# Loading the first weights at the fourth unit of attention, and handing out decode and split piece by piece

## The chip, the cores and the metric

The kernel runs on one core of one Trainium2 chip. The metric is the device time of one execution in microseconds (us). Three runs of the kernel before took 1102.81, 1103.84 and 1104.21 us; the median is 1103.84 us.

## The reference

Attention with a cumulative decay bias, causal, over 4 batches, 8 heads, 576 positions and head size 64; its output, as 2304 tokens of 512 values, goes through a gated feed-forward layer (512 to 1536 and back) and then a second one with one input matrix (512 to 2048 and back):

```
cum    = cumsum(max(s, 0))
bias   = -(cum[:, None] - cum[None, :])
scores = q @ k.T / 8 + min(bias, 0), causal mask
attn   = softmax(scores) @ v                      # (4, 8, 576, 64)
x      = attn as (2304, 512)
x      = (silu(x @ w_gate) * (x @ w_val)) @ w_out     # d_ff 1536
out    = silu(x @ w_in) @ w_out2                      # d_ff 2048
```

All is float32. The kernel keeps float32 accuracy on TensorE by splitting each matrix in a high and a low part and running three matmuls for each product (`mm3`: high times high, high times low, low times high).

## The kernel before, in words

**Attention.** A unit is one half ("A": query tiles 0 to 2, "B": tiles 3 and 4) of one head; 64 units in all. `slot_pieces(u)` lists the pieces of work of unit u: the scores and softmax of its tiles, the split of the next head, the load of the head after that, the product with v of unit u-2 and the transposes of unit u-1. The first 18 units (batch 0 and the first head of batch 1) run alone; the rest are mixed into the feed-forward layer, two units to a chunk.

**Feed-forward layers.** The weights come in chunks of 128 x 2048 values. `stream` is the list of chunks: nine for each batch in the first layer (`L1`: six of the gate and value matrices, "gv"; three of the output matrix, "o1"), then eight for the second layer. Each first-layer chunk is 96 matmuls of 288 columns, in 4 steps (gv) or 8 steps (o1). The accumulators of a gate step, the tiles `pgv`, take two of the four PSUM banks of the pool `ps_m`.

**First weights.** The weights arrive in HBM as pairs of 32-bit words, viewed from 64-bit numbers. So a chunk that is met for the first time is loaded as four tiles `r64` of 512 KB each (`w_load`), decoded to float32 (`w_decode`: per tile two ScalarE instructions, lines 413 and 414, and two VectorE instructions, lines 415 and 418), written back to HBM as float32 (`w32`, two stores of 512 KB, line 423), and split in two halves (`w_split`: per half a ScalarE copy to `wh`, line 433 through 113, and a GpSimd subtract to `wl`, line 434). In batches 1 to 3 the chunk is read back from `w32` and only split. The intermediate `dk` of the decode lies in `ps_m` too for the first nine chunks. The tiles `r64` and `wraw` share one pool of five buffers; `wh` and `wl` have four buffers each, two chunks' worth.

**When this is written.** The load, decode and split of chunk 0 and the load of chunk 1 are all written after unit 8 (`PRE = 8`, lines 585 to 589); the load stands behind the loads of the head that was asked for last. In the chunk loop `w_ahead(c)` (lines 568 to 573) writes the whole decode and split of chunk c+1 and the load of chunk c+2 ahead of the first step of chunk c.

**The order on the engines.** The program is written in this order, but a scheduler of the framework places every instruction: it lets instructions that it believes ready go ahead of ones that are written earlier and wait. The result is one fixed order for each engine, which the chip then runs in order: an instruction that waits holds all that stand behind it on its engine. All DMAs are issued from the queue of SyncE (SP).

Of the kernel before, what the change touches and what calls it, by code (L numbers as in the profile page):

```python
# [8 lines left out]
F32 = mybir.dt.float32  # L9
# [8 lines left out]
P = 128  # L18
HB = S // 2
NP = H // 2  # L20
KD = DM // P
# [37 lines left out]
PRE = 8  # L59
# [8 lines left out]
def kernel(  # L68
# [285 lines left out]
    wst = {}  # L354
# [42 lines left out]
    def w_decode(c):  # L397

        raws = []
        for e, t in enumerate(wst[c]):
            lo, hi = t[:, :, 0], t[:, :, 1]
            if e % (CW // 2 // DW) == 0:
                z = raw_p.tile([P, CW // 2], F32, tag="wraw", name="wraw")
                raws.append(z)
            o = e % (CW // 2 // DW) * DW
            zz = z[:, o : o + DW]
            if c < len(L1):
                k = ps_m.tile([P, DW], F32, tag="m", name="dk").bitcast(U32)  # L410
            else:
                k = dec_p.tile([P, DW], U32, tag="dk", name="dk")
            nc.scalar.activation(out=zz, in_=hi.bitcast(F32), func=AF.Copy, scale=2.0**-112)
            nc.scalar.activation(out=k, in_=lo, func=AF.Copy, scale=0.937 * 2.0**-29)  # L414
            nc.vector.scalar_tensor_tensor(  # L415
                out=k, in0=zz.bitcast(U32), scalar=3, in1=k, op0=ALU.logical_shift_left, op1=ALU.bitwise_or
            )
            nc.vector.scalar_tensor_tensor(  # L418
                out=zz.bitcast(U32), in0=hi, scalar=0x80000000, in1=k, op0=ALU.bitwise_and, op1=ALU.bitwise_or
            )  # L420
        for e, z in enumerate(raws if stream[c] in place else []):
            g = place[stream[c]]
            nc.sync.dma_start(out=w32[g, :, e * (CW // 2) : (e + 1) * (CW // 2)], in_=z)
        wst[c] = raws

    def w_split(c):
        if first[c]:
            w_decode(c)
        halves = []
        for t, eng, eng_h in zip(wst[c], WL[phase[c]], WH[phase[c]]):  # L430
            wh = wt_p.tile([P, CW // 2], F32R, tag="wh", name="wh")
            wl = wt_p.tile([P, CW // 2], F32R, tag="wl", name="wl")
            copy(eng_h, wh, t)
            engines[eng].tensor_tensor(out=wl, in0=t, in1=wh.bitcast(F32), op=ALU.subtract)  # L434
            halves.append((wh, wl))
        wst[c] = halves
# [242 lines left out]
```

## Time and profile before

| | |
|---|---|
| median of three runs | 1103.84 us |
| profiled execution: time | 1104.17 us |
| profiled execution: span of the trace | 1102.4 us |
| PE busy | 1073.2 us, 97% of the span |
| DVE, ACT, POOL busy | 705.1 us (64%), 587.2 us (53%), 532.7 us (48%) |
| loads of first weights `r`, 512 KB each | 52 |
| stores `w<-wraw`, 512 KB each | 18 |

The profiled execution lasted 1.8 us longer than its span; what lies outside the span isn't in the trace. A busy PE is one whose matmuls, with modelled ends, cover the time: matmuls overlap, so the row can read full while fewer of them run. The granted clock of TensorE (PEclk) is given as a share of full speed; its two levels are 2.4 GHz and 1.2 GHz. Waits are put down to the instruction whose semaphore came last.

### The profile page before, as it was taken

The numbers are of one execution on the slowest core, as the hardware profiler recorded it, in microseconds if no ns is written. First come the engines' busy times: TensorE is split into PE (matmuls) and PEld (weight loads), VectorE is DVE, ScalarE is ACT, GpSimd is POOL, SyncE is SP. The second block draws the span as 40 slices with busy tenths as digits, with TensorE's granted clock in tenths as the row PEclk, the third lists the DMA queues.
The fourth block names the chain that finished last, engine by engine and source line by source line (L and its number), as shares of the span: only waits on it lengthen the run. The fifth ranks groups of instructions, "written<-read, shape, count | busy, mean of one in ns | idle before, by whom it ended". The sixth has DMA issues, their size and how long they took to land. (4 is left out here: it accounts for less than half of the span.)

```text
span 1102.4 us, 19356 instructions
## 1 busy us (share of the span) xinstructions
PE 1073.2 (97%) x6760; PEld 994.2 (90%) x6760; DVE 705.1 (64%) x1625; ACT 587.2 (53%) x1294; POOL 532.7 (48%) x611
## 2 busy tenths in 40 slices
PE   7979899999999999999999999999999999999998
PEld 4647899999999999999999999888989898888887
DVE  6877788897778886868765346715364645644333
ACT  4887788875766564666645434655243433422221
POOL 7666677675666664757434453232323222332221
PEclk9988999999999999999999999999999999999999
DMA  5587487785353534533144223711010101000012
GB/s 135 137 242 239 157 216 239 210 250 174 86 143 90 140 95 140 149 83 101 39 154 147 77 86 123 226 41 59 20 58 20 58 20 58 20 1 1 1 61 111
DMA packets 53728, 121.39 MB, mean 110 GB/s; under 512 B 8256, under 2 KB 21568, under 8 KB 53632
## 3 DMA queue, kind: packets, MB, share of 16 engines
q1 hardware_dynamic: 53632, 120.17, 36.8%
q8 instruction: 53, 0.87, 0.3%
q14 instruction: 43, 0.35, 0.1%
HBM read 101.20 MB, written 18.95 MB: 109 GB/s over the span
## 5 line engine op out<-in xcount | busy, mean ns | idle before, releaser
L460 POOL TENSOR_TENSOR h<-u,h 128x288 fp32r<-128x288 f32 (+2 forms) x176 | 193.2, 1099 | 349.5 <-ACT h L113 344.7
L445 PE MATMUL po<-h,wh 128*128 128x288 f32 (+2 forms) x704 | 232.8, 332 | 2.1 <-ACT h L113 1.2
L446 PE MATMUL po<-h,wh 128*128 128x288 f32 (+2 forms) x704 | 232.9, 331 | 0.1
L445 PE MATMUL pgv<-xt,wh 128*128 128x288 f32 x768 | 230.9, 301 | 1.4 <-DVE u L458 0.8
L447 PE MATMUL po<-h,wl 128*128 128x288 f32 (+2 forms) x704 | 232.0, 330 | 0.0
L446 PE MATMUL pgv<-xt,wh 128*128 128x288 f32 x768 | 228.8, 298 | 1.5 <-DVE xt L349 1.5
L447 PE MATMUL pgv<-xt,wl 128*128 128x288 f32 x768 | 228.6, 298 | 0.0
L434 POOL TENSOR_TENSOR wl<-wraw,wh 128x1024 fp32r<-128x1024 f32 x53 | 129.2, 2437 | 113.8 <-ACT wh L113 101.5
L113 ACT ACTIVATE h<-u 128x288 fp32r<-128x288 f32 (+2 forms) x176 | 89.4, 508 | 118.0 <-DVE u L458 66.4
L445 PEld LDWEIGHTS pgv<-xt,wh 128*128 128x128 f32 x768 | 144.9, 189 | 3.0 <-DVE u L458 1.1
L446 PEld LDWEIGHTS pgv<-xt,wh 128*128 128x128 f32 x768 | 145.2, 189 | 2.0 <-DVE xt L349 1.8
L447 PEld LDWEIGHTS pgv<-xt,wl 128*128 128x128 f32 x768 | 145.1, 189 | 0.3
L445 PEld LDWEIGHTS po<-h,wh 128*128 128x128 f32 x704 | 132.0, 188 | 10.2 <-ACT h L113 1.8
L456 DVE SCALAR_TENSOR_TENSOR u<-th,pu 128x464 f32<-128x464 f32 (+1 forms) x80 | 50.7, 633 | 137.9 <-ACT th L454 137.9
L447 PEld LDWEIGHTS po<-h,wl 128*128 128x128 f32 x704 | 132.2, 188 | 7.0
L446 PEld LDWEIGHTS po<-h,wh 128*128 128x128 f32 x704 | 132.2, 188 | 6.9 <-POOL h L460 0.5
L540 DVE SCALAR_TENSOR_TENSOR acc<-po,acc 128x464 f32<-128x464 f32 (+1 forms) x140 | 88.5, 636 | 62.6 <-PE po L447 61.9
L454 ACT ACTIVATE th<-pu 128x464 f32<-128x464 f32 (+1 forms) x80 | 44.1, 552 | 152.2 <-PE pu L447 152.2
L113 ACT ACTIVATE wh<-wraw 128x1024 fp32r<-128x1024 f32 x88 | 92.2, 1056 | 52.0 <-PE po L446 27.1
L446 PE MATMUL pu<-x,wh 128*128 128x464 f32 (+1 forms) x320 | 118.9, 371 | 0.0
L445 PE MATMUL pu<-x,wh 128*128 128x464 f32 (+1 forms) x320 | 118.6, 371 | 0.0
L447 PE MATMUL pu<-x,wl 128*128 128x464 f32 (+1 forms) x320 | 118.5, 370 | 0.0
(87 smaller groups left out, 2012.9 us busy)
## 6 DMA issues: line engine op xcount, KB each, us to landing
wraw<-w SPq DMA_DIRECT2D x54, 512.0 KB, 4.8
r<-in_w_dram SPq DMA_DIRECT2D x52, 512.0 KB, 5.0
qkr<-in_qk_dram SPq DMA_DIRECT2D x64, 288.0 KB, 5.1
w<-wraw SPq DMA_DIRECT2D x18, 512.0 KB, 4.4
cumb<-cum_d SPq DMA_DIRECT2D x30, 288.0 KB, 4.1
r<-in_w_dram SPq DMA_DIRECT2D x32, 256.0 KB, 3.1
x_d<-acc SPq DMA_DIRECT2D x32, 144.0 KB, 3.8
vrb<-in_vb_dram SPq DMA_DIRECT2D x32, 128.0 KB, 4.6
```

Of the source, the lines that this page charges most:

```text
L113: nc.scalar.activation(out=out, in_=in_, func=AF.Copy, scale=scale)
L434: engines[eng].tensor_tensor(out=wl, in0=t, in1=wh.bitcast(F32), op=ALU.subtract)
L445: nc.tensor.matmul(out=ps[:, :n], lhsT=a, rhs=xh, start=(k == 0), stop=False)
L446: nc.tensor.matmul(out=ps[:, :n], lhsT=a, rhs=xl, start=False, stop=False)
L447: nc.tensor.matmul(out=ps[:, :n], lhsT=c, rhs=xh, start=False, stop=(k == last))
L454: nc.scalar.activation(out=th[:, :n], in_=pg[:, :n], func=AF.Tanh, scale=0.5)
L456: nc.vector.scalar_tensor_tensor(out=u, in0=th[:, :n], scalar=1.0, in1=pg[:, :n], op0=ALU.add, op1=ALU.mult)
L460: engines[LO[ph]].tensor_tensor(out=lo, in0=u, in1=hi.bitcast(F32), op=ALU.subtract)
L540: nc.vector.scalar_tensor_tensor(out=a, in0=ps[:, :n], scalar=0.5, in1=a, op0=ALU.mult, op1=ALU.add)
```

## The change

`PRE` goes from 8 to 3. `w_split` and `w_decode` are cut into pieces: a first-time chunk has six (decode of a tile, four times, and after every second one the store and split of a half), another chunk two. A new class `Spread` hands a list of pieces out over a number of steps. The pieces of chunk 0, and then the load of chunk 1, are handed out over units 4 to 8; the pieces of chunk 1 over units 11 to 15. In the loop the pieces of chunk c+1 and then the load of chunk c+2 are handed out ahead of the first steps of chunk c, so that all are out before its last step; in the second layer behind the `up2` of the first four of a chunk's five token blocks. The arithmetic stays as it is.

```
-PRE = 8
+PRE = 3
...
-    def w_decode(c):
...
+    def w_decode(c, e):
...
+    def w_half(c, e, t):
+        if first[c] and stream[c] in place:
+            nc.sync.dma_start(out=w32[place[stream[c]], :, e * (CW // 2) : (e + 1) * (CW // 2)], in_=t)
+        wh = wt_p.tile([P, CW // 2], F32R, tag="wh", name="wh")
+        wl = wt_p.tile([P, CW // 2], F32R, tag="wl", name="wl")
+        copy(WH[phase[c]][e], wh, t)
+        engines[WL[phase[c]][e]].tensor_tensor(out=wl, in0=t, in1=wh.bitcast(F32), op=ALU.subtract)
+        wsp.setdefault(c, []).append((wh, wl))
+
+    def split_pieces(c):
+
+        if not first[c]:
+            return [lambda e=e: w_half(c, e, wst[c][e]) for e in range(2)]
+        n = CW // 2 // DW
+        pcs = []
+        for e in range(CW // DW):
+            pcs.append(lambda e=e: w_decode(c, e))
+            if e % n == n - 1:
+                pcs.append(lambda e=e: w_half(c, e // n, wz[c]))
+        return pcs
...
     def w_ahead(c):
-        wst.pop(c - 1, None)
-        if c + 1 < len(stream):
-            w_split(c + 1)
+
+        wst.pop(c - 2, None)
+        wsp.pop(c - 2, None)
+        pcs = []
+        if c + 1 < len(stream) and c + 1 not in wsp:
+            pcs = split_pieces(c + 1)
         if c + 2 < len(stream):
-            w_load(c + 2)
+            pcs.append(lambda: w_load(c + 2))
+        return pcs
+
+    class Spread:
+
+
+        def __init__(self, pcs, steps):
+            self.pcs, self.steps, self.at, self.n = pcs, steps, 0, 0
+
+        def step(self):
+            self.n += 1
+            want = min(self.n, self.steps) * len(self.pcs) // self.steps
+            while self.at < want:
+                self.pcs[self.at]()
+                self.at += 1
...
             if u == PRE:
                 with tc.issue_after(loads[-1].ins):
                     w_load(0)
-                w_split(0)
-                w_load(1)
+                early = Spread(split_pieces(0) + [lambda: w_load(1)], 5)
+            if u > PRE:
+                early.step()
+            if u == PRE + 7:
+                early = Spread(split_pieces(1), 5)
...
-            k = 0
-            for n, stp in enumerate(cur):
-                if n == 0:
-                    w_ahead(c)
+            att, ahead = Spread(pcs, len(cur)), Spread(w_ahead(c), len(cur) - 1)
+            for stp in cur:
+                ahead.step()
                 stp()
...
+                att.step()
```

What the scheduler makes of it differs from the order before in one stretch only. On every engine the two orders are the same up to head 3 of batch 0, and again from the last chunk of batch 0 on.

The SP queue, at the load of chunk 0 (`r64`). `vrb` with the number 751 is the second part of v of head 6, `vrb` 346 that of head 3. Before:

```order
L189 DMA cumb_933<-cum_d_123 128x576
L192 DMA vra_750<-in_va_dram 64x64
L193 DMA vrb_751<-in_vb_dram 128x256
L389 DMA r64_780<-in_w_dram 128x1024
L389 DMA r64_782<-in_w_dram 128x1024
L389 DMA r64_784<-in_w_dram 128x1024
L389 DMA r64_786<-in_w_dram 128x1024
L174 DMA qkr_1206<-in_qk_dram 64x2x576 x2
```

With the change:

```order
L192 DMA vra_345<-in_va_dram 64x64
L189 DMA cumb_485<-cum_d_123 128x576
L193 DMA vrb_346<-in_vb_dram 128x256
L389 DMA r64_426<-in_w_dram 128x1024
L389 DMA r64_428<-in_w_dram 128x1024
L389 DMA r64_430<-in_w_dram 128x1024
L389 DMA r64_432<-in_w_dram 128x1024
L174 DMA qkr_780<-in_qk_dram 64x2x576 x2
```

The four loads have moved up by three heads. The stretch of ScalarE's order that holds the decode and split of chunks 0 and 1 moves with them: it was 49 instructions that began after the softmax of the first half of head 6, and it is 48 that begin after that of head 3, with the same 20 weight instructions in it.

The TensorE queue, at the first scores of head 5 (`psc_886`); `pgv` are gate accumulators of chunk 0, `xt` the attention output of a pair of heads. Before:

```order
L292 MATMUL ptr_874<-ident_117,e_723 128x128 x2
L242 MATMUL psc_886<-ks_738,qh_739 128x64
L242 MATMUL psc_886<-ks_738,ql_740 128x64
L242 MATMUL psc_901<-ks_738,qh_739 128x192
L242 MATMUL psc_901<-ks_738,ql_740 128x192
L242 MATMUL psc_912<-ks_738,qh_739 128x320
```

With the change:

```order
L292 MATMUL ptr_874<-ident_117,e_758 128x128 x2
L242 MATMUL psc_886<-ks_773,qh_774 128x64
L242 MATMUL psc_886<-ks_773,ql_775 128x64
L448 MATMUL pgv_1469<-xt_496,wh_664 128x288
L449 MATMUL pgv_1469<-xt_496,wh_664 128x288
L450 MATMUL pgv_1469<-xt_496,wl_665 128x288
L448 MATMUL pgv_1469<-xt_794,wh_664 128x288
L449 MATMUL pgv_1469<-xt_794,wh_664 128x288
L450 MATMUL pgv_1469<-xt_794,wl_665 128x288
L242 MATMUL psc_901<-ks_773,qh_774 128x192
```

Gate matmuls of chunk 0 now stand between the scores of head 5; before, the first of them stands behind the scores of the first half of head 8. Up to that point the new order holds 36 of them: 24 within head 5, 12 within heads 6 and 7. The four accumulators that they open take the banks that the four `dk` tiles of chunk 1 leave.

The GpSimd queue, in the chunks "gv" 1 and 2 (chunks 1 and 2): `wl` are the two halves of chunk 3, `h` the gate outputs, four to a chunk. Before:

```order
L434 TENSOR_TENSOR wl_2130<-wraw_2112,wh_2129 128x1024
L460 TENSOR_TENSOR h_2141<-u_2169,h_2141 128x288
L460 TENSOR_TENSOR h_2141<-u_2228,h_2141 128x288
L117 TENSOR_SCALAR e_2005<-e_2005,rl_2066 128x448
L117 TENSOR_SCALAR e_2051<-e_2051,rl_2066 128x576
```

With the change:

```order
L463 TENSOR_TENSOR h_2112<-u_2140,h_2112 128x288
L117 TENSOR_SCALAR e_2005<-e_2005,rl_2066 128x448
L117 TENSOR_SCALAR e_2051<-e_2051,rl_2066 128x576
L117 TENSOR_SCALAR e_2146<-e_2146,rl_2157 64x64
L117 TENSOR_SCALAR e_2161<-e_2161,rl_2226 128x192
L117 TENSOR_SCALAR e_2216<-e_2216,rl_2226 128x320
L426 TENSOR_TENSOR wl_2259<-wraw_2177,wh_2258 128x1024
L463 TENSOR_TENSOR h_2112<-u_2210,h_2112 128x288
```

The second half of chunk 3 stood ahead of the first of the four `h` of chunk 2 and now stands behind it: one step of a chunk later.

## Rows read from the trace of the kernel before

**Rows 1.** The page's slices of the span, PE, 40 slices of 27.6 us.

```profile
PE   7979899999999999999999999999999999999998
```

**Rows 2.** Windows: stretch, its length, busy us per engine, PEclk, DMA share, GB/s.

```profile
28.30:61.20 32.90, 31.73 (x175) 20.49 (x174) 26.55 (x96) 26.20 (x74) 23.37 (x45) 1.00 0.50 133
70.00:90.20 20.20, 15.35 (x57) 8.56 (x55) 13.21 (x39) 16.93 (x41) 14.12 (x21) 0.75 0.95 266
260.00:580.00 320.00, 319.66 (x2448) 315.55 (x2448) 240.13 (x639) 193.10 (x472) 187.47 (x228) 1.00 0.40 115
```

**Rows 3.** Timeline of PE: start, us, line, tiles, shape.

```profile
28.32 0.28 PE L242 MATMUL psc<-ks,qh 128*128 128x64 f32 x1
...
61.20 0.28 PE L242 MATMUL psc<-ks,qh 128*128 128x64 f32 x1
...
87.23 0.28 PE L242 MATMUL psc<-ks,qh 128*128 128x64 f32 x1
...
90.23 0.40 PE L445 MATMUL pgv<-xt,wh 128*128 128x288 f32 x1
...
90.73 0.29 PE L445 MATMUL pgv<-xt,wh 128*128 128x288 f32 x1
90.86 0.29 PE L446 MATMUL pgv<-xt,wh 128*128 128x288 f32 x1
```

**Rows 4.** Timeline of ACT; in brackets the idle time before and what ended it.

```profile
65.31 0.68 ACT L413 ACTIVATE wraw<-r 128x512 f32<-128x512 f32 x1 [0.25 <-DMA r<-in_w_dram]
...
80.25 0.64 ACT L414 ACTIVATE dk<-r 128x512 uint32<-128x512 uint32 x1 [2.27 <-DMA r<-in_w_dram]
...
96.32 1.06 ACT L113 ACTIVATE wh<-wraw 128x1024 fp32r<-128x1024 f32 x1 [2.03 <-DVE wraw L418]
...
131.01 1.22 ACT L413 ACTIVATE wraw<-r 128x512 f32<-128x512 f32 x2 [4.12 <-DMA w<-wraw]
```

**Rows 5.** Groups by line and shape: count, busy us, mean ns, idle before.

```profile
L113 ACT ACTIVATE wh<-wraw 128x1024 fp32r<-128x1024 f32 x88 | 92.2, 1056 | 52.0 <-PE po L446 27.1 <-PE pgv L446 11.6 <-DMA x_d<-acc 7.0
...
L415 DVE SCALAR_TENSOR_TENSOR dk<-wraw,dk 128x512 uint32<-128x512 uint32 x68 | 50.8, 759 | 9.7 <-ACT dk L414 5.7 <-ACT wraw L413 3.7
L413 ACT ACTIVATE wraw<-r 128x512 f32<-128x512 f32 x68 | 43.9, 667 | 21.1 <-DVE wl L434 7.6 <-DMA w<-wraw 6.3 <-issue 3.2
L414 ACT ACTIVATE dk<-r 128x512 uint32<-128x512 uint32 x68 | 43.8, 645 | 32.9 <-DMA r<-in_w_dram 29.7 <-DVE wraw L418 1.6 <-DVE u L456 1.5
```

**Rows 6.** Timeline of SP's queue: start and length of DMA issues.

```profile
35.69 0.34 SPq L193 DMA_DIRECT2D vrb<-in_vb_dram  x1
...
60.64 0.34 SPq L193 DMA_DIRECT2D vrb<-in_vb_dram  x1
61.03 1.86 SPq L389 DMA_DIRECT2D r<-in_w_dram  x4
```

**Rows 7.** Waits of PE, 60 to 260 us: total, times, longest.

```profile
PE psc L242 <- DVE x L343: 4.5, 3, 2.9
PE pgv L446 <- DVE xt L349: 1.5, 1, 1.5
```

**Rows 8.** Windows behind two of these waits.

```profile
105.00:110.00 5.00, 5.00 (x31) 5.00 (x31) 3.39 (x13) 1.99 (x7) 2.78 (x7) 0.74 0.48 121
135.00:140.00 5.00, 4.64 (x23) 4.25 (x24) 4.97 (x12) 5.00 (x11) 0.75 (x1) 0.67 0.50 147
```

**Rows 9.** Timeline of POOL and PE: a second weight half, and its chunk's first matmul.

```profile
205.10 2.40 POOL L434 TENSOR_TENSOR wl<-wraw,wh 128x1024 fp32r<-128x1024 f32 x1
...
213.68 0.40 PE L445 MATMUL po<-h,wh 128*128 128x288 f32 x1 [0.63 <-DVE wraw L418]
```

**Rows 10.** Timeline of DVE and POOL: one VectorE form, alone and beside GpSimd.

```profile
83.69 0.76 DVE L212 TENSOR_TENSOR ql<-qkr,qh 128x576 fp32r<-128x576 f32 x1 [1.03 <-ACT qh L113]
...
98.35 2.40 POOL L434 TENSOR_TENSOR wl<-wraw,wh 128x1024 fp32r<-128x1024 f32 x1
98.40 2.96 DVE L212 TENSOR_TENSOR ql<-qkr,qh 128x576 fp32r<-128x576 f32 x1
```

More of the change, by code (lines that the diff above doesn't have):

```diff
@@ L351 @@
     xin = {b: [None] * NP for b in range(B)}
-    wst = {}
+    wst, wz, wsp = {}, {}, {}
     L1 = [("gv", 0), ("gv", 1), ("gv", 2), ("o1", 0), ("gv", 3), ("gv", 4), ("o1", 1), ("gv", 5), ("o1", 2)]
@@ L395, in w_load @@
             wst[c].append(t)
-    def w_decode(c):
[L401 to L436, printed above, removed]
+    def w_decode(c, e):
+        t = wst[c][e]
+        lo, hi = t[:, :, 0], t[:, :, 1]
+        if e % (CW // 2 // DW) == 0:
+            wz[c] = raw_p.tile([P, CW // 2], F32, tag="wraw", name="wraw")
+        o = e % (CW // 2 // DW) * DW
+        zz = wz[c][:, o : o + DW]
+        if c < len(L1):
+            k = ps_m.tile([P, DW], F32, tag="m", name="dk").bitcast(U32)
+        else:
+            k = dec_p.tile([P, DW], U32, tag="dk", name="dk")
+        nc.scalar.activation(out=zz, in_=hi.bitcast(F32), func=AF.Copy, scale=2.0**-112)
+        nc.scalar.activation(out=k, in_=lo, func=AF.Copy, scale=0.937 * 2.0**-29)
+        nc.vector.scalar_tensor_tensor(
+            out=k, in0=zz.bitcast(U32), scalar=3, in1=k, op0=ALU.logical_shift_left, op1=ALU.bitwise_or
+        )
+        nc.vector.scalar_tensor_tensor(
+            out=zz.bitcast(U32), in0=hi, scalar=0x80000000, in1=k, op0=ALU.bitwise_and, op1=ALU.bitwise_or
+        )
@@ L471, in gate @@
             xs = [(t * 1024 + k * 256 + f_in * P, xin[b][k]) for k in range(KD)]
-            mm3(ps, wst[c], xs, n0, n)
+            mm3(ps, wsp[c], xs, n0, n)
             pst.append(ps)
@@ L479, in down @@
         xs = [(f * 512 + m * P, hs[4 * g + f]) for f in range(4)]
-        mm3(ps, wst[c], xs, n0, n)
+        mm3(ps, wsp[c], xs, n0, n)
         if (b, m) not in accs:
@@ L521, in up2 @@
             ps = ps_m.tile([P, 512], F32, tag="m", name="pu")
-            mm3(ps, wst[c], [(k * 256 + f * P, x2[k, t]) for k in range(KD)], 0, n)
+            mm3(ps, wsp[c], [(k * 256 + f * P, x2[k, t]) for k in range(KD)], 0, n)
             h = p2["h"].tile([P, 2, TW], F32R, tag="h2", name="h2")
@@ L532, in down2 @@
             ps = p2["ps"].tile([P, 512], F32, tag="o", name="po2")
-            mm3(ps, wst[c], [(1024 + f * 512 + m * P, hh[f]) for f in range(2)], 0, n)
+            mm3(ps, wsp[c], [(1024 + f * 512 + m * P, hh[f]) for f in range(2)], 0, n)
             if j == 0:
@@ L623, in body @@
         for i, (c, t) in enumerate(todo):
+            if t == 0:
+                ahead = Spread(w_ahead(c), len(TB) - 1)
             up2(c, t)
+            ahead.step()
             if i < 2:
@@ L628, in body @@
                 down2(*todo[i - 1])
-            if t == 0:
-                w_ahead(c)
         down2(*todo[-1])
```

4 lines of the change are left out of this document (removed).

## The prediction

> **What bounds the kernel now.** I read the page's slices first: TensorE is full from the sixth slice on and short of full before it [rows 1]. Then windows. From 260 to 580 us PE is busy 319.66 of 320 us [rows 2]; nothing done to ScalarE, VectorE or the DMAs can shorten that, only more matmuls or a wait. The orders of the two kernels agree from the last chunk of batch 0 on, so the change is decided between 40 us, where they part, and about 260 us: by how much earlier or later the common tail begins.
>
> In that stretch three things are to be seen. First, four heads of attention without weights, from the first scores of head 2 at 28.32 to those of head 6 at 61.20 us [rows 3], take 32.9 us, 8.2 us a head; in them PE is busy 96% and ACT 26.20 of 32.90 us, 80% [rows 2]. Second, heads 6 and 7, up to 87.23 us [rows 3], take 26.0 us, 9.6 us more than two heads at that pace. There the decode of chunk 0 and most of that of chunk 1 lie; ACT's stretch of it runs from 65.31 to the end of the copy at 96.32, so to 97.38 us [rows 4], 32.1 us. PE is busy 15.35 of 20.20 us in its middle, at a mean clock of 0.75, with DMA at a share of 0.95 [rows 2]. Third, after the feed-forward work begins at 90.23 us [rows 3], PE waits now and then for attention work that came late: 1.5 us for `xt`, and 4.5 us in three waits for `x`, the longest 2.9 us [rows 7]. Behind the first and behind the longest, stretches follow in which the mean clock is 0.74 and 0.67 [rows 8], so part of them runs at 1.2 GHz.
>
> **The change part by part.** The arithmetic and its instructions stay: each first chunk has eight decode instructions on ACT, eight on DVE, two copies on ACT, two subtracts on POOL, four loads and two stores. They move.
>
> *The block of chunks 0 and 1 moves three heads up.* The loads stand behind `vrb` of head 3, which issued at 35.69, in place of that of head 6 at 60.64 us; the first decode instruction ran 4.67 us after the latter [rows 4, 6], so I expect it at 40.4 us. In the block ACT runs 8 x 0.667 + 8 x 0.645 + 4 x 1.056 = 14.7 us for weights [rows 5]. Before, the last 7 us of the block lay beside feed-forward matmuls; now all of it lies in attention. What it costs there: in the 32.1 us of the block ACT waited 2.27 and 2.03 us [rows 4], which leaves 27.8 us; less 14.7 that is 13.1 us of attention, which at 80% is 16.5 us of attention's pace. So the block costs 32.1 - 16.5 = 15.6 us with both waits, and 11.3 us with neither. The first wait is for a weight load behind other transfers, in the same order as now, and should recur; the second is for a VectorE that was also serving the gates, and should not. I take 13.6 us. DVE is less full: 81% of 16.5 us and 16 instructions of 0.76 us (the row is of the first of each pair, the second taken as long) [rows 2, 5] are 25.5 us, under ACT's 27.8. POOL, 71% of 16.5 us and four subtracts of 2.40 us [rows 2, 9], has 21.3 us. Of the 13.6 us, 9.6 were paid before. The loads of chunk 2 and its first two decode instructions now also stand ahead of the gates: 1.3 us of ACT, which I take as 1.0 since ACT is 80% full. Sum of the part: 13.6 - 9.6 + 1.0 = +5.0 us. Bounds: +1.7 (no wait, the extra hidden) and +7.3 (both waits, nothing hidden).
>
> *36 gate matmuls go ahead.* A gate matmul takes 0.13 us, 90.73 to 90.86 us [rows 3], so 36 are 4.7 us that PE need not do after the attention. 24 of them stand in the block, where PE has slack, 3.1 us; 12 in heads 6 and 7, where PE is 96% busy [rows 2] and I count half, 0.8 us. That is -3.9 us, bounds -3.1 and -4.7.
>
> *Chunk 0 has no decode of its successor beside it.* With it should go the wait of 1.5 us for `xt` [rows 7] and the slow clock behind it, (1 - 0.74) x 5 = 1.3 us [rows 8]: -2.8 us, bounds 0 and -2.8.
>
> *Chunks 1 to 7: the same work in smaller bits.* The waits for `x`, 4.5 us [rows 7], and the slow clock behind the longest, (1 - 0.67) x 5 = 1.7 us [rows 8], are what a perfect spread could win: -6.2 us. The longest followed 4.12 us in which ACT stood at a decode that needed the buffer of a store still under way [rows 4]. In the new order that buffer's store and the next decode are nearer together, but less else is in the DMA queues when the store issues. ACT is strictly in order, so a wait there holds the softmax and the gates. I take a third of the gain, -2.0 us; bounds -6.2 and +3, the latter one more wait and its slow clock of the size seen (2.9 us).
>
> *What costs nothing:* the second layer and the later batches, whose orders don't change.
>
> Sum: +5.0 - 3.9 - 2.8 - 2.0 = -3.7 us. On the profiled execution, 1104.17 us (its span of 1102.4 and 1.8 around it), that is 1100.5; the median of the runs is 0.3 us lower, so 1100.1, and I predict 1100 us.
>
> One row speaks of a price that I have in no term. The subtract for `ql` takes 0.76 us on DVE, and 2.96 us where it began 0.05 us after a weight subtract of 2.40 us on POOL [rows 10]. The Trainium skill says why ("SBUF — State Buffer", section "Who interferes with whom"): a VectorE instruction with two SBUF inputs and a GpSimd instruction that reads SBUF cannot run together, and the later one blocks until the other is done. The row agrees. By that rule each of the two weight subtracts that move from the gates into attention could hold DVE by 2.2 us there, up to +4.4 us, and the sum would be +0.7; but two of the four already stood in attention before and are in the 32.1 us, and the same wait leaves chunk 0.
>
> **The rivals.** *A: the spread works in full.* All waits for `x` go, and the block runs without ACT waits: +1.7 - 4.7 - 2.8 - 6.2 = -12.0, 1092 us. For it: the waits seen follow bursts of decode. Against it: the stores and loads keep their order, so the DMA waits should come back.
>
> *B: nothing is left over.* The block costs its upper end, the 12 gates in heads 6 and 7 win nothing, and new waits in chunks 1 to 7 replace the old: +7.3 - 3.1 - 2.8 + 0 = +1.4, 1105 us. For it: DMA is at a share of 0.95 in the block [rows 2], and with 3 MB more (loads of chunk 2, stores of chunk 1) ahead of the gates the loads of heads 7 and 8 come later. Against: these loads have about two heads of lead.
>
> *C, slower: the second half of the weights comes late.* Spread over the steps, it is subtracted one step later. Before, POOL ended it for the chunk that begins at 213.68 us at 207.50 [rows 9], 6.2 us ahead. A step of a gate chunk is about 213.68 - 90.23 = 123.5 us over six chunks and four steps, 5.1 us [rows 3, 9]. So about 1 us is left, and where ACT or POOL fall behind by more than that, PE stands at the chunk's first matmuls. If it stands 1.5 us at each of six starts, with the slow clock behind half of them (3 x 1.5 us), that is +13.5, and with the gain in chunks 1 to 7 gone the sum is -1.7 + 13.5 = +11.8: 1116 us; at 0.5 us a start and no slow clock it is +1.3. It decides from a lead of zero. For it: every piece is handed out as late as one step before its use. Against: the first half, which is needed first, keeps most of its lead.
>
> **How the numbers follow.** The forecast has a chance of 0.50, A 0.15, B 0.15, C 0.20. What a measurement of this kernel can tell from no change is 0.2%, 2.2 us. The forecast's own range, from one or two terms off by half their bounds, is 1096 to 1104: 0.40 of its 0.50 lie over 2.2 us faster, 0.10 within. A is faster; B is 0.11 within and 0.04 slower; C is 0.02 within and 0.18 slower. Faster 0.55, same 0.23, slower 0.22. The range for 8 in 10 leaves out the far half of A and the far half of C: 1091 to 1109.
>
> **What would show it.** The first decode instruction of chunk 0 on ACT near 40 us. The stretch to the last `wh` of chunk 1 near 30 us long, and the head in it slower than 8.2 us by 13 to 14 us in all. Gate matmuls between the scores of head 5. The first gate matmul that is no forerunner near 95 us, not 90. No wait of 1.5 us for `xt` in chunk 0. From then on PE full but for short waits. The step on the block is wrong if the heads lose under 10 or over 17 us. The forecast is wrong if ACT waits longer for weight loads or stores than the 2.27 and 4.12 us seen, or if PE's waits at the first matmul of a chunk name the weights' `wl` or `wh`.

## Result and profile after

The changed kernel takes 1119.3 us (median of 4 runs, 1118.9 to 1119.8), the kernel before 1104.0 us beside it. The ratio is 1.014, 95% interval 1.0123 to 1.0158: slower by 1.4%, where I had forecast 1100 us and a range up to 1109. The span of the profiled execution is 1116.6 us, 14.2 more than before.

The page's slices of the kernel after, PE and the granted clock, answer to [rows 1]:

```profile
PE   6779999988999999999999999999999999999998
...
PEclk9989999999999999999999999999999999999999
```

The second slice (28 to 56 us) reads 7 where it was 9, and the ninth and tenth (223 to 279 us) read 8 where PE had been full.

To see where the 14 us arose I read from PE's timeline when each chunk's first matmul with `wl` runs; call that the chunk's begin (of chunk 1 on, since a part of chunk 0's now runs ahead). Chunk 1 begins at 116.5 us before and 120.8 after, chunk 4 at 175.2 and 178.8, chunk 7 at 232.0 and 240.5, chunk 9 at 265.8 and 279.9, and from there on the two kernels stay 13.9 to 14.7 us apart. So 4.3 us arose ahead of chunk 1, -0.7 in chunks 1 to 3, 4.9 in chunks 4 to 6, and 5.6 in chunks 7 and 8. Windows between these begins, columns as in [rows 2], first of after:

```profile
28.65:66.68 38.03, 28.48 (x129) 17.78 (x130) 27.12 (x82) 28.26 (x70) 21.90 (x35) 0.82 0.76 223
66.68:98.95 32.27, 28.58 (x169) 20.29 (x167) 24.60 (x77) 24.42 (x65) 22.04 (x35) 1.00 0.63 190
98.95:120.80 21.85, 20.49 (x146) 17.80 (x145) 18.32 (x62) 17.68 (x47) 15.21 (x31) 1.00 0.41 106
120.80:178.80 58.00, 55.83 (x416) 53.79 (x415) 50.40 (x133) 46.26 (x109) 41.41 (x54) 1.00 0.71 215
178.80:240.50 61.70, 57.56 (x423) 55.74 (x422) 54.29 (x141) 46.68 (x107) 41.03 (x51) 0.97 0.67 207
240.50:279.90 39.40, 34.53 (x243) 32.86 (x242) 34.50 (x72) 22.70 (x51) 21.37 (x24) 0.96 0.68 199
```

and of before:

```profile
116.50:175.20 58.70, 54.72 (x404) 52.54 (x403) 46.25 (x126) 45.44 (x107) 40.90 (x50) 0.97 0.74 213
175.20:232.00 56.80, 55.21 (x420) 53.60 (x419) 52.61 (x145) 47.39 (x110) 42.61 (x53) 1.00 0.75 222
232.00:265.80 33.80, 33.80 (x258) 33.26 (x258) 29.09 (x76) 21.26 (x51) 22.39 (x26) 1.00 0.77 230
```

The first number behind the length is PE's busy time. In the last stretch PE was full before; after, it stands 4.87 of 39.40 us and runs part of the rest at 1.2 GHz (mean clock 0.96). VectorE's busy time there rose from 29.09 to 34.50 us with 4 instructions fewer: some of them took longer.

What was foreseen came for the most part where it was looked for. ScalarE's first decode ran at 40.94 us (foreseen 40.4, [rows 4] before). Two groups of 12 gate matmuls ran inside attention, at 67.7 and 74.3 us, and 12 more matmuls between 85.3 and 93.8. The wait of 1.5 us for `xt` in chunk 0 is gone, and from head 8's first scores to chunk 1 the kernel takes 21.9 us (98.95 to 120.80) where it took 29.3 (87.23 in [rows 3] to 116.5): 7.4 us won, foreseen 3.9 + 2.8 = 6.7. But head 8 begins 11.7 us late, not 5.0. ScalarE's waits for DMA, its timeline with the idle time in brackets, answering to [rows 4]:

```profile
40.94 0.68 ACT L411 ACTIVATE wraw<-r 128x512 f32<-128x512 f32 x1 [0.82 <-DMA r<-in_w_dram]
...
43.50 0.68 ACT L411 ACTIVATE wraw<-r 128x512 f32<-128x512 f32 x1 [1.07 <-DMA r<-in_w_dram]
...
56.84 0.63 ACT L412 ACTIVATE dk<-r 128x512 uint32<-128x512 uint32 x1 [2.38 <-DMA r<-in_w_dram]
60.29 0.63 ACT L412 ACTIVATE dk<-r 128x512 uint32<-128x512 uint32 x1 [2.43 <-DMA r<-in_w_dram]
...
177.03 0.64 ACT L412 ACTIVATE dk<-r 128x512 uint32<-128x512 uint32 x1 [2.74 <-DMA r<-in_w_dram]
...
179.54 1.26 ACT L411 ACTIVATE wraw<-r 128x512 f32<-128x512 f32 x2 [1.16 <-DMA w<-wraw]
```

The first four stand in the block of chunks 0 and 1, 6.7 us where the term let one of 2.27 recur: two at chunk 0's loads, two at chunk 1's. Before, chunk 1's decode followed chunk 0's as directly, and besides the wait of 2.27 us it had one more for its loads:

```profile
82.42 0.63 ACT L414 ACTIVATE dk<-r 128x512 uint32<-128x512 uint32 x1 [0.76 <-DMA r<-in_w_dram]
```

PE's large waits after the change, its timeline:

```profile
54.72 0.65 PE L292 MATMUL ptr<-ident,e 128*64 128x128 f32 x3 [2.83 <-POOL e L117]
...
61.26 0.63 PE L242 MATMUL psc<-ks,qh 128*128 128x320 f32 x1 [3.87 <-ACT ph L113]
...
262.95 0.46 PE L242 MATMUL psc<-ks,qh 128*128 128x320 f32 x1 [3.13 <-DVE pl L310]
```

The first is for attention's `e`, which GpSimd scales right behind a weight subtract of 2.35 us (51.69 to 54.04); the second is for a `ph` that ScalarE copied only behind the second of its two waits for chunk 1's loads. Clock windows at and behind these waits:

```profile
54.96:65.20 10.24, 6.37 (x21) 4.08 (x20) 5.66 (x10) 5.42 (x11) 6.13 (x8) 0.50 0.79 256
...
263.20:266.60 3.40, 3.40 (x16) 3.40 (x16) 3.30 (x12) 1.88 (x4) 0.00 (x0) 0.50 0.16 58
```

Both are wholly at 1.2 GHz. The same heads, 3 to 7, as a whole, first after, then before:

```profile
36.60:98.95 62.35, 49.26 (x255) 32.92 (x253) 45.92 (x137) 46.35 (x115) 38.26 (x59) 0.89 0.72 219
```

```profile
36.25:87.23 50.98, 44.44 (x218) 27.60 (x217) 38.46 (x131) 42.06 (x108) 33.91 (x58) 0.90 0.74 210
```

They take 11.4 us more. PE stands 13.1 us in them where it stood 6.5, and its busy time rose by 4.8 us, about the length of the 36 gate matmuls that now stand there (4.7 us in the prediction). The mean clock is nearly the same, since heads 6 and 7 ran partly at 1.2 GHz before too.

The wait at 262.95 leads back to one VectorE instruction. The timeline of VectorE and GpSimd there:

```profile
255.65 6.91 DVE L349 TENSOR_TENSOR xt<-x,xt 128x320 fp32r<-128x320 f32 x1
262.48 1.00 DVE L310 TENSOR_TENSOR pl<-ptr,ph 64x256 fp32r<-64x256 f32 x2
...
255.33 0.93 POOL L117 TENSOR_SCALAR e<-e,rl 128x192 f32<-128x192 f32 x2
256.23 2.38 POOL L426 TENSOR_TENSOR wl<-wraw,wh 128x1024 fp32r<-128x1024 f32 x1
258.56 0.81 POOL L463 TENSOR_TENSOR h<-u,h 128x288 fp32r<-128x288 f32 x1
259.32 0.59 POOL L234 TENSOR_SCALAR_AFFINE_SELECT e<-cumb 128x256 f32<-128x256 f32 x2
259.87 2.34 POOL L426 TENSOR_TENSOR wl<-wraw,wh 128x1024 fp32r<-128x1024 f32 x1
```

A subtract of 0.48 us at its shortest took 6.91: it ended 0.35 us after GpSimd had run out of work (259.87 + 2.34 = 262.21). `pl` was queued behind it, and PE behind `pl`. Before, the two weight subtracts of that chunk ran back to back and well ahead of `xt`. The corresponding place:

```profile
235.24 5.34 POOL L434 TENSOR_TENSOR wl<-wraw,wh 128x1024 fp32r<-128x1024 f32 x2 [2.12 <-ACT wh L113]
...
249.95 2.40 POOL L434 TENSOR_TENSOR wl<-wraw,wh 128x1024 fp32r<-128x1024 f32 x1
...
248.92 0.61 DVE L349 TENSOR_TENSOR xt<-x,xt 128x320 fp32r<-128x320 f32 x1 [0.54 <-ACT xt L113]
```

That `xt` took 0.61 us, and the next weight subtract began 0.4 us after its end. Over the first batch the 128x320 form, grouped by line and shape from 36 to 290 us, before:

```profile
L349 DVE TENSOR_TENSOR xt<-x,xt 128x320 fp32r<-128x320 f32 x7 | 4.3, 616 | 0.5 <-ACT xt L113 0.5
```

and after:

```profile
L349 DVE TENSOR_TENSOR xt<-x,xt 128x320 fp32r<-128x320 f32 x7 | 15.7, 2247 | 5.9 <-ACT xt L113 5.9
```

### The profile page after: what moved, and what is told of

Its sections match the earlier page's. It is cut to its first block, busy times and chain, and to the rows that moved or that the text cites. A ratio compares the mean times of both kernels' runs of the same rounds, so it can differ in the third digit from the quotient of the medians.

```text
span 1116.6 us, 19344 instructions
## 1 busy us (share of the span) xinstructions
PE 1075.3 (96%) x6760; PEld 994.8 (89%) x6760; DVE 716.0 (64%) x1625; ACT 587.6 (53%) x1294; POOL 531.7 (48%) x611
## 5 line engine op out<-in xcount | busy, mean ns | idle before, releaser
L113 ACT ACTIVATE h<-u 128x288 fp32r<-128x288 f32 (+2 forms) x176 | 89.3, 507 | 114.9 <-DVE u L461 63.8
L449 PE MATMUL pu<-x,wh 128*128 128x464 f32 (+1 forms) x320 | 118.8, 371 | 0.0
```

The source lines that it names most:

```text
L113: nc.scalar.activation(out=out, in_=in_, func=AF.Copy, scale=scale)
L449: nc.tensor.matmul(out=ps[:, :n], lhsT=a, rhs=xl, start=False, stop=False)
```

## Experiments

All the kernels in one table. "In one go" and "spread" say how decode and split are given out in the loop; the unit is the one after which chunk 0's weights are loaded; the last three columns are of one profiled execution each, which can lie off the kernel's median (by 4.5 us for "spread, unit 8", 2.5 us for "in one go, unit 4", -2.7 us for "`xt` operand in PSUM"). The ratios are against the kernel before, run on the same chip (medians 1103.2 to 1105.0).

| kernel | us | ratio, 95% | chunk 1 begins | 1 to 7 | 7 to 9 |
|---|---|---|---|---|---|
| before: in one go, unit 8 | 1104.0 | | 116.5 | 115.5 | 33.8 |
| after: spread, unit 3 | 1119.3 | 1.0123 to 1.0158 | 120.8 | 119.7 | 39.4 |
| in one go, unit 3 | 1108.8 | 1.0025 to 1.0052 | 120.0 | 117.6 | 33.9 |
| spread, unit 8 | 1107.4 | 1.0005 to 1.0040 | 115.3 | 124.0 | 34.6 |
| in one go, unit 4 | 1108.5 | 1.0023 to 1.0053 | 123.4 | 115.9 | 34.6 |
| spread, unit 4 | 1117.2 | 1.0077 to 1.0144 | 120.0 | 123.8 | 37.8 |
| in one go, unit 7 | 1120.8 | 1.0118 to 1.0198 | 121.0 | 129.0 | 32.9 |
| spread, unit 7 | 1111.2 | 1.0050 to 1.0100 | 119.4 | 123.5 | 30.7 |
| after, one chunk's stores only | 1108.9 | 1.0032 to 1.0069 | 117.4 | 114.5 | 37.0 |
| after, `xt` operand in PSUM | 1115.2 | 1.0082 to 1.0116 | 118.8 | 122.0 | 33.6 |
| both of these | 1109.0 | 1.0028 to 1.0067 | 121.3 | 114.8 | 34.4 |
| after, half of `wl` on VectorE | 1111.7 | 1.0043 to 1.0086 | 121.7 | 117.1 | 33.7 |
| after, chunk 1's loads late | 1105.8 | 1.0003 to 1.0035 | 116.7 | 115.5 | 33.7 |
| after, `xt` on GpSimd | 1102.5 | 0.9959 to 0.9999 | 120.1 | 111.9 | 32.4 |
| the same, unit 4 | 1101.8 | 0.9953 to 0.9986 | 116.9 | 114.5 | 32.9 |
| the same, unit 8 | 1103.8 | 0.9981 to 1.0014 | 117.6 | 115.5 | 33.5 |
| the same, unit 3, chunk 1's loads late | 1107.7 | 1.0014 to 1.0035 | 123.1 | 114.9 | 33.0 |
| before, `xt` on GpSimd | 1115.0 | 1.0086 to 1.0121 | 119.4 | 125.2 | 32.9 |
| in one go, unit 3, `xt` on GpSimd | 1114.1 | 1.0076 to 1.0136 | 116.9 | 123.2 | 34.9 |
| before, `xt` operand in PSUM | 1115.1 | 1.0077 to 1.0112 | 115.0 | 125.6 | 34.6 |

**Half of the change at a time.** First the kernel before with one number changed:

```
-PRE = 8
+PRE = 3
```

> Early start alone: the first weights are loaded after unit 3, as in the changed kernel, but every later chunk's decode and split are given out in one go ahead of the chunk's first step, as before. Theory S (the loss has two separate parts, read from the chunk starts: about 4.3 us before chunk 1 from the block in attention, about 9.8 us between chunks 3 and 8 from the spread): 1104 + 4.3 = 1108.3, range 1106.5 to 1110. Rival R (the later loss follows from the early start, whatever the spread: the same weights stand with other attention work beside them): 1117 to 1120. Chunk 1's first matmul with wl at 120 to 121 us by both.

Measured 1108.8 us, chunk 1 at 120.0. So far that is S: the early start by itself costs 3.8 us. Then the changed kernel with the start as before:

```
-PRE = 3
+PRE = 8
...
-                early = Spread(split_pieces(0) + [lambda: w_load(1)], 5)
-            if u > PRE:
-                early.step()
-            if u == PRE + 7:
-                early = Spread(split_pieces(1), 5)
+                for p in split_pieces(0):
+                    p()
+                w_load(1)
```

> Spread alone: weights of chunk 0 loaded after unit 8 and decoded in one go there, as before; from chunk 0 on the pieces of the next chunk are given out between the steps, as in the changed kernel. Theory S: 1104 + 9.8 = 1113.8, range 1111 to 1116.5. Rival R: 1103 to 1106. By S the chunk starts fall behind those of the kernel before between 155 and 280 us and not earlier.

Measured 1107.4, below S's range and a little above R's. The two halves cost 3.8 and 2.4 us over what the kernel before took beside them, together they cost 15.3: so S falls, the loss is not the sum of two prices. The chunks fell behind at other places, too: here chunks 1 to 7 took 124.0 us, and 7 to 9, where the changed kernel loses most, 34.6 (in an execution of 1111.9 us).

**The held subtract.** First by moving it:

```
-            nc.vector.tensor_tensor(out=xp[:, 1], in0=x[:, :n], in1=xp[:, 0].bitcast(F32), op=ALU.subtract)
+            eng = nc.gpsimd if b < 2 else nc.vector
+            eng.tensor_tensor(out=xp[:, 1], in0=x[:, :n], in1=xp[:, 0].bitcast(F32), op=ALU.subtract)
```

> The changed kernel, with the subtract that makes the low half of xt (128x320, three operands in SBUF) on GpSimd in place of VectorE for the first two batches; the arithmetic is the same. In the changed kernel these 16 subtracts take 20.2 us on VectorE, 8.8 before, the longest 6.91 us while two weight subtracts ran on GpSimd. Theory L (VectorE held by GpSimd makes most of the 9.8 us in the loop): 6 to 10 us come back, 1109 to 1113, and no PE wait of 3 us at 259. Theory D (ScalarE standing at decode instructions for loads and stores makes it): 1117 to 1121, with the waits of ScalarE at 177, 217 and 240 us still there. If GpSimd itself becomes late with xt: above 1121, with PE waits that name POOL xt.

(The 16 subtracts of 20.2 and 8.8 us are those of 128x320 in all four batches; the edit moves eight of them, and eight of 128x256.) Measured 1102.5 us: more than L asked, 16.8 us back. PE stands 2.5 us between chunks 1 and 9, in the changed kernel 11.2 (length less busy time of the three windows). This kernel's windows, chunks 1 to 4, 4 to 7, 7 to 9:

```profile
120.10:174.60 54.50, 54.18 (x413) 53.09 (x412) 43.14 (x125) 46.76 (x110) 42.25 (x57) 1.00 0.72 225
174.60:232.00 57.40, 55.95 (x420) 54.05 (x419) 51.72 (x140) 47.65 (x109) 42.75 (x54) 1.00 0.74 220
232.00:264.40 32.40, 31.68 (x240) 30.97 (x239) 27.19 (x65) 20.29 (x46) 23.00 (x26) 1.00 0.82 239
```

No half clock is left in them. But one edit that gives back more than the whole loss may have done it by another order: the scheduler rearranged the loop on every engine. So the same edit on three other kernels:

> The kernel before, with xt's subtract on GpSimd for the first two batches, as a control for the same edit on the changed kernel (1119.3 to 1102.5). Theory L (the edit gives back what GpSimd's weight subtracts took from VectorE, and that mainly happens with the spread): before, the 16 subtracts take 8.8 us, some 2 us over their own length, so 1101 to 1105. Rival W (VectorE is short of time everywhere, and the edit wins by taking its work away): as large a gain as on the changed kernel, under 1095.

> Early start with the burst (1108.8), with xt's subtract on GpSimd. Theory L: the burst has few such meetings from 100 us on, so at most 3 us: 1105.5 to 1109. Rival W: under 1097.

> Late start with the spread (1107.4), with xt's subtract on GpSimd. Of the two PE waits for pl that this kernel showed (3.7 us at 175, 3.4 us at 229, each with a half clock behind it) the second followed a VectorE subtract held 2.6 us by a weight subtract of GpSimd, but that was vsb and not xt; the first followed two waits of ScalarE for loads. Theory L: xt's longest subtract there took 4.17 us, so 3 to 5 us back: 1102 to 1105. If the loads decide: 1106 to 1109.

1115.0, 1114.1 and 1103.8 us. The third is what L expected. The first two were made slower, by 10.6 and 5.3 us, which neither theory allows. VectorE's own share of work cannot be what matters (W), or they would have won; nor is the edit a plain refund of held time (L). In the first, ScalarE waited 6.05 us for a store at 216 us and 3.07 us for a load at 193; in the second 12.7 us in all for stores between 117 and 275 us. Then another way to thin out the meetings, which gives VectorE more work and not less:

```
-WL = ["gg", "gg", "gg", "gv"]
+WL = ["gg", "gg", "gv", "gv"]
```

> The changed kernel with the second half's weight subtract on VectorE in place of GpSimd in the first batch: nine GpSimd subtracts of 2.4 us fewer, nine VectorE ones of 1.2 us more. Theory L (what costs is VectorE held while GpSimd runs its weight subtract): VectorE meets half as many, its own 11 us more notwithstanding: 1106 to 1114. Rival W (VectorE lacks time): 1120 to 1127.

1111.7 us, chunks 7 to 9 in 33.7 us: 7.6 us back with some 11 us of work added to VectorE. W falls.

The next edit leaves the subtract on its engine and takes the second SBUF operand away. `acc` is the tile `pv` in PSUM, so the low half of `xt` gets other values:

```
-            nc.vector.tensor_tensor(out=xp[:, 1], in0=x[:, :n], in1=xp[:, 0].bitcast(F32), op=ALU.subtract)
+            src = x if whole or b > 1 else acc
+            nc.vector.tensor_tensor(out=xp[:, 1], in0=src[:, :n], in1=xp[:, 0].bitcast(F32), op=ALU.subtract)
```

> The changed kernel, with the first operand of xt's subtract read from the PSUM tile pv in place of the SBUF tile x, where pv has 128 rows, for the first two batches: the same engine and size, but other values, so the low half of xt is not the reference's. Where VectorE's subtract has an operand in PSUM the trace shows it at its own length beside a weight subtract of GpSimd (decode, pl, x). Unlike the move to GpSimd this leaves the instruction where it was, and the order of each engine nearly as it was. Theory L: the 16 subtracts fall from 20.2 to 7 to 8 us, the PE wait of 3.1 us at 259 and the half clock behind it go, 1107 to 1114. Theory O (the move to GpSimd won 17 us by the other order that it brought, not by the lock): 1117 to 1121.

1115.2 us. The edit reaches only the subtracts of batch 1, since `whole` holds in all of batch 0; up to 136 us the kernel is the changed one, instruction for instruction, and from there its order differs too. Two rows show the effect of the operand by itself, the same subtract, begun while a weight subtract of GpSimd ran, first in the changed kernel, then with the operand in PSUM:

```profile
172.31 2.13 DVE L349 TENSOR_TENSOR xt<-x,xt 128x320 fp32r<-128x320 f32 x1 [0.88 <-ACT xt L113]
...
171.71 2.39 POOL L426 TENSOR_TENSOR wl<-wraw,wh 128x1024 fp32r<-128x1024 f32 x1
```

```profile
174.37 0.49 DVE L350 TENSOR_TENSOR xt<-pv,xt 128x320 fp32r<-128x320 f32 x1
...
172.49 2.39 POOL L427 TENSOR_TENSOR wl<-wraw,wh 128x1024 fp32r<-128x1024 f32 x1
```

Then the subtract that had taken 6.91 us with what GpSimd ran beside it, and the windows of chunks 4 to 7 and 7 to 9.

```profile
256.81 0.47 DVE L350 TENSOR_TENSOR xt<-pv,xt 128x320 fp32r<-128x320 f32 x1
...
256.62 0.80 POOL L464 TENSOR_TENSOR h<-u,h 128x288 fp32r<-128x288 f32 x1
```

```profile
180.20:240.80 60.60, 55.69 (x408) 54.12 (x407) 55.91 (x140) 45.85 (x106) 39.49 (x50) 0.97 0.69 208
240.80:274.40 33.60, 33.37 (x254) 32.62 (x254) 29.57 (x76) 22.10 (x52) 21.03 (x24) 1.00 0.75 228
```

Chunk 7 begins at 240.8 us, as in the changed kernel (240.5), and from there the two part: 33.6 us to chunk 9 in place of 39.4, PE all but full and at full clock. The weight subtract stood ahead of `xt` in this order, but GpSimd's row went on without a break from 254.27 to 262.79 us, and `xt` was not held. This stretch is what L expected: 5.8 us, of which the wait of 3.1 us and the half clock behind it (half of 3.4 us) are 4.8. The stretch ahead of it is not: 60.6 us against 61.7. The whole gain in time, 4.2 us, is just short of L's range, and some of chunk 1 to 7's meetings only moved: two `vsb` subtracts, 0.41 and 0.89 us in the changed kernel, took 2.3 and 2.4 us there. The control:

> The same edit on the kernel before, as a control (low half of xt not the reference's). Theory L: the 16 subtracts take 8.8 us there, so there is little to give back: 1101 to 1105, whereas the move to GpSimd made it 10.6 us slower by its other order. Theory O would have no reason for a difference between this kernel and the changed one: both within 3 us of their own time.

1115.1 us. Neither L nor O expected that: an operand read from another place in some subtracts, where hardly anything was held, made the kernel before 10.8 us slower. What the edit changes besides is the order of the loop, from 136 us on. So 1104 us looks like one order's time, too.

**The stores.** The stores of chunks 1 to 8 left out:

```
-            nc.sync.dma_start(out=t, in_=w32[g, :, e * (CW // 2) : (e + 1) * (CW // 2)])
+            nc.sync.dma_start(out=t, in_=w32[0, :, e * (CW // 2) : (e + 1) * (CW // 2)])
...
-        if first[c] and stream[c] in place:
+        if c == 0:
             nc.sync.dma_start(out=w32[place[stream[c]], :, e * (CW // 2) : (e + 1) * (CW // 2)], in_=t)
```

> The changed kernel without the stores of the decoded weights of chunks 1 to 8 (16 stores of 0.5 MB); the later batches load chunk 0's weights for every chunk, so the output is that of other weights. A decode then never waits for a store to leave its buffer, and the loads of the next chunk have fewer transfers beside them. In the changed kernel ScalarE waits 9.6 us for loads and stores between 158 and 280 us, before 4.1 us in the whole first layer. Theory D: 4 to 10 us come back, 1109 to 1115, and ScalarE's waits for DMA after 158 us are under 2 us in all. Theory L: 1117 to 1120.

1108.9 us, at the edge of what D expected: chunk 1 begins 3.4 us earlier, and chunks 1 to 7 take 114.5 us, 5.2 less. ScalarE waits 0.97 us for loads of weights after 158 us, as D asked; by the rows these waits and those for stores are 10.1 us in the changed kernel between 158 and 280 us and 6.3 in the first layer of the kernel before, where the expectation has 9.6 and 4.1. Yet the last stretch stays long, with the same held subtract. The timeline of VectorE and PE in this kernel, and its window of chunks 7 to 9:

```profile
245.89 6.30 DVE L349 TENSOR_TENSOR xt<-x,xt 128x320 fp32r<-128x320 f32 x1
...
252.57 0.42 PE L242 MATMUL psc<-ks,qh 128*128 128x320 f32 x1 [2.40 <-DVE pl L310]
```

```profile
231.90:268.90 37.00, 34.00 (x243) 32.83 (x242) 32.48 (x71) 20.84 (x48) 22.29 (x24) 0.95 0.59 183
```

Both edits together:

> Both at once on the changed kernel: xt's subtract with an operand in PSUM, and the weights of chunks 1 to 8 not stored (the output is that of other weights and of another low half of xt). Without the stores 5.2 us came back between chunks 1 and 7 and 3.4 before chunk 1; without the hold 5.8 between 7 and 9. If they add up: chunk 1 to 7 in 113 to 116 us, 7 to 9 in 33 to 35, time 1102 to 1106. If the stores' gain was only another order: chunk 1 to 7 over 118 us, time 1107 or more.

The stretches add up as expected, 114.8 and 34.4 us. The time does not, 1109.0 us: chunk 1 begins at 121.3 us, 3.9 us later than with the stores alone left out. That isn't the order's doing: up to 133 us the two kernels run the same instructions in the same order. The changed kernel and the one with `xt`'s operand in PSUM, alike up to 136 us, began chunk 1 at 120.8 and 118.8 us. So the start of chunk 1 scatters by up to some 4 us from one profiled execution to another (here also from chip to chip), and the 3.4 us earlier start without the stores may be no more than that. In the loop two losses are told apart: chunks 4 to 6 go with the stores (61.7 and 60.6 us with them, 56.2 and 56.2 without), chunks 7 and 8 with the held subtract. How the stores do it is not settled. ScalarE's waits at 177 and 180 us are gone without them, but the order changes as well from chunk 4 on, and the kernel before has all its stores and takes 56.8 us there.

**The early block.** Chunk 1's loads held back by three heads:

```
-                early = Spread(split_pieces(0) + [lambda: w_load(1)], 5)
+                early = Spread(split_pieces(0), 5)
...
+            if u == PRE + 5:
+                with tc.issue_after(loads[-1].ins):
+                    w_load(1)
```

> The changed kernel, with chunk 1's loads held back until unit 8, three heads later, so that its decode is no longer in one block with chunk 0's. In the changed kernel ScalarE waits 2.4 us twice for chunk 1's loads in the block, and TensorE waits 2.8 and 3.9 us and runs 10.2 us at half clock there. Theory T (the block's excess of some 7 us over my forecast are these waits and their half clock): chunk 1 begins at 113.5 to 117 us in place of 120.8. Rival N (the work of two decodes costs what it costs, wherever it stands): 119.5 to 122. The time: 1112 to 1116 by T if the later losses stay, 1118 to 1121 by N; the loop's order changes too, so the start of chunk 1 decides and not the time.

> The fastest kernel so far (the changed one with xt's subtract on GpSimd, 1102.5) with chunk 1's loads held back in the same way. Theory T: 1096 to 1100. Rival N: 1101 to 1105.

The first began chunk 1 at 116.7 us, 4.1 earlier than the changed kernel, within T's range. Its timeline has the wait behind GpSimd's weight subtract still, and the one of 3.87 us not (the next long one is 0.86):

```profile
53.55 0.52 PE L292 MATMUL ptr<-ident,e 128*64 128x128 f32 x3 [2.79 <-POOL e L117]
...
61.30 0.36 PE L242 MATMUL psc<-ks,qh 128*128 128x192 f32 x1 [0.86 <-ACT x L113]
```

Its loop also fell into a better order, and the time, 1105.8, is that of both. The second went against T: chunk 1 at 123.1 us, 3.0 later than without the edit, and 1107.7 us, outside the ranges of T and N. With the scatter of some 4 us seen above, one start that came 4.1 us earlier and one that came 3.0 later leave T unproven: that the wait of 3.87 us went is shown, that it costs these 4.1 us is not.

**How far the order alone goes.** Loads shifted by one unit, here `PRE` 4 in place of 3:

> The changed kernel with the first weights loaded one unit later (after unit 4). Each engine's order is that of the changed kernel from the end of the early block on, so only the early part moves. Theory P (the losses in the loop belong to the order of its instructions and the transfers beside them): chunk 1 to 7 takes 118 to 121 us and chunk 7 to 9 38 to 40 us again, with xt's subtract near chunk 8 held over 5 us; the time 1114 to 1121, by where chunk 1 begins. Rival Q (they are chance meetings that depend on how the early part ends): either stretch differs by over 3 us from the changed kernel's 119.7 and 39.5.

Here the orders of all engines equal those of the changed kernel from the end of the early block on. The subtract was held to the same hundredth, and PE waited behind it:

```profile
258.54 6.91 DVE L349 TENSOR_TENSOR xt<-x,xt 128x320 fp32r<-128x320 f32 x1
...
265.84 0.41 PE L242 MATMUL psc<-ks,qh 128*128 128x320 f32 x1 [3.15 <-DVE pl L310]
```

Chunks 7 to 9 took 37.8 us (39.4), 1 to 7 took 123.8 (119.7), the time is 1117.2. By the bound I had set, P holds for the held subtract and Q for the stretch ahead of it. The wait of 3.15 us was followed by no half clock here (mean clock 1.00 from 243.8 to 281.6 us, 0.96 in the changed kernel's stretch), which is about the 1.6 us by which chunks 7 to 9 were shorter. The other two shifts, `PRE` 7 in the kernel before and 4 in the fastest:

> The kernel before with the first weights loaded one unit earlier (after unit 7). The scheduler's order of the loop changes in many small places. If the burst is worth its lead whatever the order: 1102 to 1107. If the order's small differences decide, as they seem to in the other kernels: anything from 1100 to 1116, with chunk 1 to 7 off its 115.5 us by more than 3.

> The fastest kernel (the changed one with xt's subtract on GpSimd, 1102.5) with the first weights one unit later. If its gain is a property of that placement: 1099 to 1105. If it was one lucky order: 1106 to 1115.

The kernel before with its loads one unit earlier takes 1120.8 us, as long as the changed one and outside both ranges that I had given. Its windows of chunks 1 to 4 and 4 to 7 show no single culprit, 8.9 us of PE standing and mean clocks of 0.94 and 0.93:

```profile
121.00:185.90 64.90, 60.59 (x419) 57.16 (x418) 49.62 (x137) 49.69 (x116) 42.35 (x55) 0.94 0.63 188
185.90:250.00 64.10, 59.48 (x409) 56.37 (x408) 54.70 (x138) 45.46 (x105) 41.24 (x51) 0.93 0.65 196
```

The fastest kernel kept its time under the same shift, 1101.8, though its order in the loop is another one. Both take 0.2 to 0.3% less than the kernel before (intervals in the table); they are not told apart from each other. The last two runs complete four pairs of in one go and spread:

> Decode and split in one go, first weights loaded after unit 4 (its pair with the spread: 1117.2). If the spread costs about 10 us in itself: 1105 to 1110. If the order's small differences decide: anything from 1102 to 1121, and no sign that holds over the four pairs.

> Decode and split spread, first weights loaded after unit 7 (its pair in one go: 1120.8). If the spread costs about 10 us in itself: 1125 to 1132. If the order's small differences decide: anything from 1102 to 1121.

1108.5 and 1111.2 us. In one go against spread: at unit 3 1108.8 and 1119.3, at 4 1108.5 and 1117.2, at 7 1120.8 and 1111.2, at 8 1104.0 and 1107.4. Three pairs are slower spread, one is 9.6 us faster. At units 3 and 4, where the loop's order is the same in both kernels of a kind, both the times and chunks 1 to 9 come out alike: in one go 151.5 and 150.5 us, spread 159.1 and 161.6. So a given order has its price, within some 3 us for chunks 1 to 9 (4.1 for the single stretch of chunks 1 to 7), and orders of the same arithmetic range from 144 us (spread, `xt` on GpSimd) to 162 (in one go, unit 7).

## Why the prediction was wrong

*That the change is decided between 40 and some 260 us, and the tail costs nothing:* right; the difference is 14.1 us at chunk 9 and 14.2 in the span.

*The gates ahead and chunk 0 without decode, -3.9 and -2.8:* right in sum, -7.4 measured over the stretch in which both lie.

*The block three heads up, +5.0, bounds +1.7 and +7.3:* wrong in size, +11.7. The failing step is "I take 13.6 us" for the block. Heads 3 to 7 took 21.3 us more than five at 8.2 (36.60 to 98.95 us), beyond the 17 us at which the prediction calls the step wrong. I let one wait of 2.27 us for a load recur; there were four, 6.7 us; why they were longer than before isn't shown. And I worked the block out from ScalarE's time alone; GpSimd's weight subtract in front of attention's `e` gave PE a wait of 2.83 us that stood in no term. The stretch of 10.24 us at 1.2 GHz that followed is hardly part of the excess, since the mean clock of heads 3 to 7 is 0.89 against 0.90; PE standing 6.5 us longer and being busy 4.8 us longer are. The 24 forerunners that I put into PE's slack there so look paid for; that is worked out from the sums and not tested. Nor is the size firm: chunk 1 began between 117.4 and 121.3 us in kernels that share this block (one chunk's stores left out in two of them).

*Chunks 1 to 7 in smaller bits, -2.0, bounds -6.2 and +3:* wrong in sign and size, +9.8 over chunks 1 to 8. "I take a third of the gain" supposed that the loop's waits are due to bursts and thin out with them. They are meetings of single instructions in one given order, and the change drew a new order. Of the 9.8, 5.6 lie in chunks 7 and 8, where one subtract was held 6.91 us; in the only three kernels in which it was held over 6 us this stretch took 37.0 to 39.4 us, in the other 17 it took 30.7 to 34.9. Some 5 us in chunks 4 to 6 went with the stores, by a way left open; chunks 1 to 3 gave 0.7 back. The bounds were wrong as well: they were taken from the waits that this one order had shown, and the kernel before is among the better of its neighbours (1108.5, 1108.8 and 1120.8 us in one go).

*The price that I had in no term:* [rows 10] showed a VectorE subtract held beside a weight subtract, and I set its price aside by counting only the two subtracts that move into attention. In the loop the change took the two subtracts of each chunk apart, so that they meet more of VectorE's work: the 128x320 `xt` subtracts from 36 to 290 us took 4.3 us before and 15.7 after. This is no draw of one order: at units 3, 4, 7 and 8 they took 6.0, 5.9, 5.8 and 4.3 us in one go and 15.7, 16.6, 9.7 and 7.9 spread. What it costs in time is the order's: at unit 7 the spread kernel was the faster all the same. Holds in the loop are what should have been a term. The Trainium skill ("SBUF — State Buffer", section "Who interferes with whom") says that a VectorE instruction with two SBUF inputs contends with a GpSimd instruction that reads SBUF, and calls the shared ports "an exclusive lock". The trace agrees, and the row at 255.65 us shows how long that can last: 6.4 us, through a row of seven GpSimd instructions.

*The rivals:* the time came near C's 1116, but not by C's mechanism: behind the forerunners' 0.65 and 1.60 us no gate waited for its weights for more than 0.32 us. B let new waits take the place of the old at no cost; they came to 9.8 us more. No rival named the order.

## What to carry to other kernels

Where a scheduler sets the order of each engine, one change is one draw: run it at a few neutral shifts (here the unit after which a load is issued) before its effect is called its own, and do not take a wait's price from one order as the bound for the next. Profile more than one execution before a difference of a few microseconds in one stretch is called an effect: here chunk 1 began up to 3.9 us apart behind the same instructions in the same order. Price a known hold at each place in which the new order brings the two engines together, not only at the block that moves. A bulk subtract on GpSimd next to short VectorE subtracts of two SBUF operands is worth taking apart, by an operand in PSUM or by giving the short one to GpSimd, but measure it with the order it brings.

## What the hardware showed unexpectedly

A VectorE subtract with two SBUF operands was held not by one GpSimd instruction but by an unbroken row of them: 6.91 us (6.30 in another kernel) for a subtract of 0.47, ending 0.35 us after the row did. Not every hold lasts so long: the one of 2.13 us at 172.31 ended 0.34 us after the weight subtract, while GpSimd went on to 174.89 us. With one operand in PSUM the subtract took 0.49 us inside a weight subtract. A small form with one tensor was held as well: `l`, 128x2, ran 2.34 us where it began 0.03 us after a weight subtract of 2.35 us (spread, unit 4); half of the `l` of this form in that kernel take 0.17 us or less:

```profile
59.92 2.34 DVE L269 TENSOR_SCALAR l<-l 128x2 f32<-128x2 f32 x1
...
59.89 2.35 POOL L426 TENSOR_TENSOR wl<-wraw,wh 128x1024 fp32r<-128x1024 f32 x1 [2.87 <-ACT wh L113]
```

The time of one kernel scatters more than the changed kernel's four runs show, which lay within 0.9 us: those of its shift by one unit, with the same order in the loop, lay between 1114.1 and 1119.8 us, those of the one with `xt` on GpSimd between 1098.4 and 1107.4.
